# A written-out engine order, rewritten for its first third: casts and copies on other engines, transfers and tiles as they were

## The chip, the cores and the metric

The kernel runs on one core of one Trainium2 chip. The metric is device microseconds of that core for one launch; lower is better. The kernel before was timed three times.

## What is computed

Windowed attention with a few global keys, and behind it a two-layer block with a softplus. B, H, S, D are 4, 8, 768, 64; the model width is 512 and the inner width 2048.

```python
scores = scale * q @ k.T + bias          # bias: -slope[h] * distance
keep   = (key < 8) | (0 <= row - key < 96)
a      = softmax(where(keep, scores, -1e9))
x      = (a @ v) as [3072, 512]          # heads side by side
h      = x @ w_in                        # [3072, 2048]
g      = max(h, 0) + log1p(exp(-|h|))    # softplus
out    = g @ w_out                       # [3072, 512], float32
```

## The kernel before

**Work and names.** The 3072 tokens are 24 blocks of 128. Two neighbouring blocks are a unit (12 units, `UNITS`, line 147); two blocks in the order of work are also a group g of 256 tokens for the second half (12 groups). Every piece of work is a small operation with a name:

- `ldq`, `ldk`, `ldv`, `win`, `wout` load a unit's q, k, v or a piece of the weights (all on SP's queue but the two halves of the first q, on ACT's). `castq`, `castk`, `castv` (lines 650 to 710) and `cin`, `cout` (line 644) turn what was loaded from float32 into bf16. `castv2.11` is the last quarter of unit 2's v.
- `trq`, `trk` transpose a unit's q and k: units 0 to 2 on TensorE with copies `cpq`, `cpk` behind it (lines 777 to 821), later units by a DMA from SP's queue (lines 823 to 838).
- Block n: `sc` scores (line 950), `z` adds the bias on DVE (line 976), `ex` is the exponential on ACT (line 983), `pv` the product with v (line 1002, in two parts), `nm` divides by the sum (lines 1013 and 1014), `xt` transposes the result (line 1033 on TensorE with the copy `xc`, line 1038, for blocks 0 to 5, and from block 6 on a DMA from SP's queue, line 1045). `gk` and `gv` (lines 846 to 871) copy the keys and values of the 8 global tokens into the previous block's tile, where `pv` reads them; `gv4.0` and `gv4.1` do so for block 4.
- Group g: `a{g}.{0..7}` is the product with w_in (line 1060, eight matmuls each), `e` the exponential (line 1075), `ln` the logarithm of 1 + e (line 1086). For groups 0 and 1 the product with w_out is `b{g}.{half}.{0,2,..14}` (line 1107, two matmuls each) and `oc` copies it out. From group 2 on it is made of seven products of half size, `b{g}.1` to `b{g}.7` (line 522), from differences of g (`ka`, line 452) and from sums of weights (`ws{p}.{j}`, line 417, 20 of them, made once).
- `fill0` to `fill34` (line 1234) are matmuls on a blank tile whose result nobody reads.

**What sets the order.** `ORDER` (lines 68 to 145) lists all 1042 operations, each with the letter of its engine (P TensorE, V DVE, A ACT, G POOL, S SP). `Program.in_order` walks through this list and issues each operation; each engine executes its own in that order, and waits where an input is not ready or a buffer is still read. Some operations may stand on more than one engine, and the letter decides:

```python
if alts:
    o.eng = self.placed[name]
    assert o.eng in alts, (name, o.eng)
    o.fn = lambda: fn(o.eng)
assert o.eng == self.placed[name], name
```

**Buffers that the steps below touch.** PSUM has two score buffers (`s_ps`, two banks each) and one bank each in `x_ps`, `o_ps`, `h_ps0`, `h_ps1`. The products `b0.1.*` collect in a bank of the second score buffer, `b0.0.*` in one of the first, so that `b0.1.0` cannot start before `z5.1` has read the scores of block 5 out of it, nor `b0.0.0` before `z5.0` has. There are three `z` buffers, so that `z5.1` also waits for the exponential that reads the buffer it takes.

Of the kernel before, what the change touches and what calls it, by code (L numbers as in the profile page):

```python
# [68 lines left out]
ldv0:S iota:G ldq0.0:A blank:V fill0:P ldk0.0:S table:A ldq0.1:A ident:G dl1a:V fill1:P dl0a:V ldk0.1:S dl0b:V fill2:P
ones:G dl1c:V dl0c:V fill3:P d0:G fill4:P d0e:V ldk1.0:S fill5:P fill6:P biasFalse5:G biasFalse3:V dl1e:V ldq1.0:S  # L70
fill7:P biasTrue0:V biasTrue3:A biasFalse1:G biasTrue5:V ldq1.1:S fill8:P biasTrue6:A ident_q:G fill9:P biasTrue7:V
castv0.01:A ldk1.1:S biasFalse6:G biasFalse7:V fill10:P biasTrue1:A biasTrue4:V castv0.11:G fill11:P ldv1:S
biasFalse2:V biasFalse0:A fill12:P castq0.0:A fill13:P fill14:P biasFalse4:V ident_p:G castk0.0:V biasTrue2:A fill15:P
# [5 lines left out]
cpk1.0:V fill28:P cpk1.1:A xt1:P cin0:V win6:S fill29:P sc2.0:P cin1:A fill30:P z2.1:V fill31:P win7:S z2.0:V xc1:A
cin3:G castv1.10:V ex2.0:A sc3.0:P fill32:P a0.0:P z3.0:V wout0:S cin2:G wout1:S pv2.0:P fill33:P e0.0:A a0.1:P  # L80
nm2.0:V wout2:S castq2.0:G ex2.1:A z3.1:V castq2.1:G a0.2:P ldv2:S e0.1:A castk2.0:G pv2.1:P castk2.1:V trq2.0:P
e0.2:A nm2.1:V wout3:S trk2.0:P ex3.0:A cin5:G cpq2.0:V xt2:P cpk2.1:V a0.3:P xc2:V cpk2.0:A cpq2.1:V pv3.0:P ex3.1:A
cin4:G fill34:P nm3.0:V sc4.0:P ln0.0:A pv3.1:P gk5:G a0.4:P nm3.1:V cin6:G e0.3:A z4.0:V xt3:P e0.4:A a0.5:P cin7:G
ln0.1:A wout4:S z4.1:V a0.6:P xc3:A cout0:G e0.5:A wout5:S sc5.0:P e0.6:A a0.7:P ex4.0:A z5.0:V cout1:G ldq3:S a1.0:P
e0.7:A ldk3:S z5.1:V b0.0.0:P e1.0:A a1.1:P cout2:V ex4.1:A ws0.4:V b0.1.0:P castv2.11:G castv2.01:A b0.0.2:P wout7:S
castv2.00:V b0.1.2:P e1.1:A gv4.1:G ws0.1:V a1.2:P ln0.2:A pv4.0:P ws0.6:V a1.3:P e1.2:A nm4.0:V cout3:A b0.0.4:P
ws1.1:V pv4.1:P e1.3:A a1.4:P cout4:V wout6:S ln0.3:A ws0.3:V ldv3:S a1.5:P gv5.1:V nm4.1:V ln1.0:A b0.1.4:P cout5:V
xt4:P ex5.0:A b0.0.6:P castq3.0:V b0.1.6:P ws2.6:V b1.0.0:P trq3:S e1.4:A b0.1.8:P ws1.4:V ln1.1:A b1.0.2:P ws1.7:V
b0.0.8:P e1.5:A xc4:V b1.0.4:P ws2.1:V castv2.10:A b0.1.10:P ex5.1:A a1.6:P gv5.0:V cout7:V ldq4:S cout6:V a1.7:P
castk3.0:A ws1.3:V b0.1.12:P e1.6:A trk3.0:S ws0.7:V b0.1.14:P ln1.2:A pv5.0:P ws2.7:G ws2.4:V b0.0.10:P b0.0.12:P  # L90
gk6:A ldk4:S nm5.0:V e1.7:A b1.0.6:P trk3.1:S oc0.1.0:V pv5.1:P ln1.3:A b0.0.14:P castv3.00:G nm5.1:V b1.0.8:P ws2.3:V
oc0.0.0:A b1.0.10:P castv3.01:A xt5:P ldv4:S sc6.0:P xc5:V castq4.0:A gv6.0:V b1.0.12:P gv6.1:V z6.0:V b1.0.14:P
castv3.10:A trq4:S a2.1:P oc1.0.0:A castk4.0:G z6.1:V ex6.0:A a2.0:P ldq5:S ws1.6:G trk4.0:S pv6.0:P ex6.1:A b1.1.0:P
nm6.0:V b1.1.2:P gk8:A gk7:V pv6.1:P e2.0:A ws3.3:V sc7.0:P gv7.1:G e2.1:A nm6.1:V ldk5:S a2.2:P gv7.0:G z7.0:V
ln2.0:A xt6:S a2.3:P castv4.10:G e2.2:A z7.1:V castv3.11:G b1.1.4:P ex7.0:A gv8.1:G b1.1.6:P trk4.1:S gv8.0:V b1.1.8:P
ws3.4:G e2.3:A pv7.0:P ex7.1:A sc8.0:P nm7.0:V st0.0.0:S a2.5:P castq5.0:G z8.0:V ln2.1:A pv7.1:P b1.1.10:P
castv4.01:G trq5:S e2.5:A nm7.1:V a2.4:P castv4.11:G ex8.0:A z8.1:V castv4.00:G a2.7:P xt7:S e2.4:A gk9:G ws3.6:V
ex8.1:A pv8.0:P castk5.0:G b1.1.12:P st0.1.0:S nm8.0:V a2.6:P ldv5:S e2.7:A ws3.7:V ldq6:S ln2.2:A b1.1.14:P trk5.0:S
pv8.1:P oc1.1.0:V sc9.0:P e2.6:A gv9.1:G ws3.1:V a3.1:P ln2.3:A gv9.0:G z9.0:V a3.0:P e3.1:A ka2.6:G z9.1:V b2.3:P
e3.0:A ldk6:S ex9.0:A b2.4:P nm8.1:V gk10:G ex9.1:A ka2.7:V a3.2:P xt8:S pv9.0:P e3.2:A a3.3:P ldv6:S nm9.0:V oe2.a:A  # L100
trk5.1:S ka2.2:V a3.4:P e3.3:A ka2.1:V ln3.0:A pv9.1:P sc10.0:P nm9.1:V gv10.0:G e3.4:A a3.5:P z10.1:V castq6.0:G
xt9:S b2.1:P e3.5:A gk11:G ka2.5:V ldq7:S castv5.00:G ex10.1:A a3.6:P trq6:S oe2.1:V castv5.01:G a3.7:P gv10.1:V
e3.6:A castv6.01:G z10.0:V ln3.1:A b2.5:P castv5.11:G st1.0.0:S e3.7:A ldk7:S b2.2:P castk6.0:V ex10.0:A trk6.0:S
sc11.0:P oe2.c:V a4.0:P castq7.0:G z11.1:V pv10.0:P e4.0:A castv5.10:G b2.7:P nm10.0:V trk6.1:S ln3.3:A castv6.11:G
z11.0:V a4.2:P ln3.2:A pv10.1:P trq7:S a4.1:P gv11.0:G e4.2:A ka3.6:V gv11.1:G b2.6:P e4.1:A st1.1.0:S nm10.1:V
ex11.0:A a4.4:P castv6.00:G ka3.2:V xt10:S castk7.0:G a4.3:P e4.4:A oe2.7:V ldv7:S sc12.0:P e4.3:A ka3.1:G trk7.0:S
pv11.0:P z12.1:V b3.3:P ex11.1:A nm11.0:V a4.5:P ln4.0:A z12.0:V pv11.1:P e4.5:A a4.6:P nm11.1:V ex12.0:A castv6.10:V
# [1281 lines left out]
```

## Time and profile before

| what | value |
|---|---|
| median of 3 runs | 211.15 us (211.12 to 211.19) |
| the profiled execution | 211.24 us, of it 209.3 us from first to last instruction |
| TensorE (PE) busy | 201.7 us of 209.3 |
| ACT, DVE, POOL busy | 169.9, 156.2, 115.8 us |
| longest links of the chain that ended last | `a` products 33%, seven-product `b` 25% of the span |
| the DMA link in that chain | v of unit 2, 11.38 us |

In the profile's rows a line stands for an operation's kind (L644 is a weight cast, L707 a cast of v, L868 `gv`, and so on), buffer numbers are left out, and what is in square brackets is the idle time of the engine ahead of an instruction and what ended it. PEld is the weight load that runs beside the matmuls. SPq rows are issues of DMAs by SP. The span has three stretches: up to about 28 us the weights and the first units arrive and TensorE also does fillers; from there to about 66 us groups 0 to 2 run beside the last weight pieces; behind that, the seven-product groups.

### The profile page before, as it was taken

The page shows a single profiled execution, that of the slowest core. Times are in us where ns is not written, and L with a number is a line of the kernel's source. Part 1 is how long each engine was busy: PE and PEld are TensorE (multiplying, and loading weights), DVE is VectorE, ACT ScalarE, POOL GpSimd, SP SyncE. Part 2 cuts the span into 40 slices and gives each one's busy share as a digit, 9 for nine tenths or more (in the row PEclk, how much of TensorE's full clock was granted, in tenths as well). Part 3 has the DMA queues.
Part 4 walks back from the last instruction along what each step waited for, and adds up shares of the span by engine and source line. Part 5 has one row for each costly group of instructions (what it writes and reads, how often), then busy time and mean ns, then how long its engine had stood idle before and what let it go on. Part 6 is the DMA issues. An engine that isn't in the chain of part 4 may idle for free.

```text
span 209.3 us, 5513 instructions
## 1 busy us (share of the span) xinstructions
PE 201.7 (96%) x2211; PEld 164.8 (79%) x2211; DVE 156.2 (75%) x293; ACT 169.9 (81%) x239; POOL 115.8 (55%) x131
## 2 busy tenths in 40 slices
...
GB/s 175 364 362 388 388 358 360 332 241 209 220 244 206 253 203 308 172 203 302 197 196 255 200 164 232 188 142 125 103 75 43 111 5 129 74 0 0 103 20 182
DMA packets 70649, 40.99 MB, mean 196 GB/s; under 512 B 30432, under 2 KB 62688, under 8 KB 70624
## 3 DMA queue, kind: packets, MB, share of 16 engines
...
HBM read 27.26 MB, written 6.29 MB: 160 GB/s over the span
## 4 chain that ended last, share of the span: by engine, by line
PE 75%; DMA 12%; DVE 4%; ACT 3%; POOL 2%; SPq 1%; issue 1%; DVEq 0%; ACTq 0%; POOLq 0%
PE h_ps L1060 33%; PE o_ps L522 25%; DMA raw<-in_v_dram 7%; DMA raw<-in_moe_w_in_dram 5%; PE x_ps L1002 5%; PE s_ps L950 4%; PE s_ps L1107 2%; PE o_ps L1107 2%; PE x_ps L522 2%; PE s_ps L522 1%; DVE z L976 1%; POOL vb L707 1%; DVE raw L417 1%; ACT vb L707 1%; SPq L640 1%
## 5 line engine op out<-in xcount | busy, mean ns | idle before, releaser
L1060 PE MATMUL h_ps<-XT,w_in_bf 128*128 128x256 bf16 x768 | 94.6, 273 | 0.0
L1060 PEld LDWEIGHTS <-w_in_bf 128*128 128x128 bf16 x768 | 73.1, 98 | 10.9 <-POOL w_in_bf L644 0.3
L1075 ACT ACTIVATE e<-h_ps 128x512 f32<-128x512 f32 x96 | 60.0, 637 | 18.8 <-PE h_ps L1060 18.2
L1086 ACT ACTIVATE g<-e 128x1024 bf16<-128x1024 f32 x48 | 49.6, 1050 | 0.5
L976 DVE TENSOR_TENSOR z<-s_ps,biasA 128x1024 f32<-128x1024 f32 x38 | 45.9, 1219 | 4.3 <-PE s_ps L950 3.4
L983 ACT ACTIVATE pb<-z 128x1024 bf16<-128x1024 f32 (+1 forms) x44 | 43.2, 990 | 1.1 <-DVE z L976 1.0
L452 POOL TENSOR_TENSOR g<-g 128x1024 bf16<-128x1024 bf16 x11 | 23.8, 2171 | 22.0 <-DVE raw L452 21.8
L522 PEld LDWEIGHTS <-g 128*128 128x128 bf16 x320 | 30.8, 98 | 3.7
L452 POOL TENSOR_TENSOR raw<-g 128x1024 bf16<-128x1024 bf16 x9 | 19.6, 2176 | 14.4 <-ACT g L1086 12.9
L522 PEld LDWEIGHTS <-raw 128*128 128x128 bf16 x240 | 22.6, 98 | 2.8
L707 POOL CAST vb<-raw 64x512 bf16<-64x512 f32 x29 | 20.9, 724 | 7.0 <-DMA raw<-in_v_dram 5.8
L522 PE MATMUL o_ps<-raw,raw 128*128 128x256 bf16 x192 | 24.3, 273 | 0.0
L452 DVE TENSOR_TENSOR raw<-g 128x1024 bf16<-128x1024 bf16 x21 | 16.2, 780 | 6.5 <-ACT g L1086 4.1
L1002 PEld LDWEIGHTS <-pb 128*128 128x128 bf16 x352 | 16.6, 98 | 5.3 <-issue 1.9
L522 PE MATMUL o_ps<-raw,g 128*128 128x256 bf16 x160 | 19.6, 273 | 0.0
L868 POOL COPY vb<-vb 4x512 bf16<-4x512 bf16 x21 | 13.8, 657 | 7.8 <-PE x_ps L1002 5.8
L1014 DVE TENSOR_TENSOR xs<-x_ps,rcp 128x256 bf16<-128x256 f32 x40 | 17.0, 425 | 1.4
L1002 PE MATMUL x_ps<-vb,pb 128*128 128x65 bf16 x304 | 16.0, 194 | 1.3 <-POOL vb L868 0.9
L522 PE MATMUL o_ps<-w_out_bf,g 128*128 128x256 bf16 x128 | 15.8, 273 | 0.0
L675 POOL CAST qb<-raw 128x1024 bf16<-128x1024 f32 (+1 forms) x10 | 9.8, 989 | 7.5 <-DMA raw<-in_q_dram 7.3
L1234 PE MATMUL x_ps<-blank 128*128 128x512 bf16 x35 | 12.4, 476 | 1.2 <-DVE blank L1159 1.2
L1013 DVE RECIPROCAL rcp<-x_ps 128x4 f32<-128x4 f32 x40 | 7.1, 177 | 8.5 <-PE x_ps L1002 8.1
...
## 6 DMA issues: line engine op xcount, KB each, us to landing
...
raw<-in_moe_w_in_dram SPq DMA_DIRECT2D x8, 512.0 KB, 10.1
...
```

Source lines behind the costliest of these rows:

```text
L452: (nc.vector if eng == "DVE" else nc.gpsimd).tensor_tensor(dst, a[0], b[0], ALU.subtract)
L522: nc.tensor.matmul(psum(j), lhs[:, f // 2, f % 2, :], w(f), start=(f == 0 and not (chain and j in "267")), stop=(f == 7), skip_group_check ...
L707: copy_on[eng](dst, src)
L868: copy_on[eng](vb_of(prev)[sl, :, 0:D], vb_of(first)[sl, :, 0:D])
L976: nc.vector.tensor_tensor(z, src, bias, ALU.add)
L983: nc.scalar.activation(pb[:, 0:nr, :].rearrange("p (y a) b -> p y (a b)", y=2), src, AF.Exp, scale=1.0 / root_d)
L1002: nc.tensor.matmul(xv[:, h, :], pb[:, 4 * (h % 2) + 2 * part + h // 2 if lone else u_all * (2 * (h % 2) + h // 2) + u, :], vb_of(prev if u ...
L1014: nc.vector.tensor_tensor(xs[:, 4 * part : 4 * part + 4, :], xv[:, :, 0:D], rcp[:][:, :, None].to_broadcast([P, 4, D]), ALU.mult,)
L1060: last = nc.tensor.matmul(hv[:, j, :], w_in_bf[:, m, fb * P : fb * P + P], XT[g % NXG][:, m, :], start=(m == 0), stop=(m == NM - 1),)
L1075: nc.scalar.activation(e[:, p % 2, :, :].rearrange("p j (b t r) -> p (j b) r t", b=2, r=2), hb[:].rearrange("p (a r t) -> p a r t", a=4, r=2),
L1086: nc.scalar.activation(gt[:, 2 * p - 2 : 2 * p + 2, :].rearrange("p a t -> p (a t)"), e[:].rearrange("p a j t -> p (a j t)"), AF.Ln, bias=1.0,
L1234: nc.tensor.matmul(x_ps[:], blank[:, 0:P], blank[:])
```

## The change

The text of `ORDER` is another list for its first 39 lines, and some neighbours are swapped in ten lines further down; all other code is the same. The same 1042 operations stand in it. Up to about block 8 of 24 they come in another order on PE, DVE, ACT and POOL, and 62 of them stand on another engine. SP's own order is the same, operation for operation; on ACT's queue the two halves of the first q change places. All 35 fillers are kept, the first 14 where they were. One line of the list, before and after:

```diff
-ex1.1:A gk4:G ldq2.0:S pv0.0:P fill18:P nm0.0:V fill19:P fill20:P ldq2.1:S fill21:P castq1.0:A pv0.1:P fill22:P
+castv0.10:A win2:S fill17:P fill18:P ex0.1:A castk1.1:G ldq2.0:S sc1.0:P fill19:P ldq2.1:S ex1.1:A pv0.0:P fill20:P
```

The 62 operations that change engines, by kind: 10 biases, both identity permutations, 17 casts of q, k and v, 12 weight casts (`cin0`, `cin1` to POOL, `cin3` to ACT, `cin4`, `cin5`, `cin7` to DVE; `cout2`, `cout4`, `cout5`, `cout6` to POOL, `cout3` to DVE, `cout7` to ACT), 9 copies out of PSUM, 3 `gk` and 3 `gv` copies (`gv4.1` to DVE) and 6 `ws` (`ws0.3`, `ws2.3`, `ws2.4`, `ws3.7` to POOL, `ws1.6`, `ws2.7` to DVE).

On POOL, from `cin4` (the first row) on, before; L852 is `gk5`, the two L644 ahead of L707 are `cout0` and `cout1`, L707 is `castv2.11`, L868 `gv4.1` and L417 `ws2.7`:

```order
L644 CAST w_in_bf<-raw_77 128x2x512
L852 COPY kT_88<-kTa_91 128x4x8
L644 CAST w_in_bf<-raw_67 128x2x512
L644 CAST w_in_bf<-raw_79 128x2x512
L644 CAST w_out_bf<-raw_72 128x1024
L644 CAST w_out_bf<-raw_73 128x1024
L707 CAST vb<-raw_74 64x8x64
L868 COPY vb<-vb 4x8x64
L417 TENSOR_TENSOR raw_73<-raw_77 128x512
```

The same place on POOL after; L852 is `gk5`, L868 is now `gv4.0`, the L644 from raw_72 on are `cout0`, `cout1`, `cout2`, `cout4`, `cout5`, `cout6`, and the L417 between them is `ws0.3`:

```order
L644 CAST w_in_bf<-raw_67 128x2x512
L852 COPY kT_88<-kTa_91 128x4x8
L868 COPY vb<-vb 4x8x64
L644 CAST w_out_bf<-raw_72 128x1024
L644 CAST w_out_bf<-raw_73 128x1024
L417 TENSOR_TENSOR raw_70<-raw_72,raw_73 128x512
L644 CAST w_out_bf<-raw_80 128x1024
L644 CAST w_out_bf<-raw_76 128x1024
L644 CAST w_out_bf<-raw_77 128x1024
L644 CAST w_out_bf<-raw_78 128x1024
L417 TENSOR_TENSOR raw_73<-raw_76,raw_77 128x512 x2
```

Unit 2's v and `gv4.1` have left POOL, and five weight pieces and three `ws` have come to it.

On DVE, around the scores of blocks 4 and 5 (`z4.0`, `z4.1`, `z5.0`, `z5.1` are the four L976), before; L644 is `cout2`, the L417 are `ws0.4`, `ws0.1`, `ws0.6` and L707 is `castv2.00`:

```order
L976 TENSOR_TENSOR z_95<-s_ps_61,biasA 128x1024
L976 TENSOR_TENSOR z_96<-s_ps_62,biasA 128x1024
L976 TENSOR_TENSOR z_94<-s_ps_61,biasA 128x1024
L976 TENSOR_TENSOR z_95<-s_ps_62,biasA 128x1024
L644 CAST w_out_bf<-raw_80 128x1024
L417 TENSOR_TENSOR raw_70<-raw_72,raw_73 128x512
L707 CAST vb<-raw_74 64x8x64
L417 TENSOR_TENSOR raw_70<-raw_72,raw_73 128x512
L417 TENSOR_TENSOR raw_70<-raw_72 128x512
```

The same place on DVE after; the first L644 is `cin7`, L868 is `gv4.1`, the L417 are `ws0.1`, `ws0.6`, the L707 are `castv2.01`, `castv2.00` and then `castv2.11`, the second L644 is `cout3`:

```order
L644 CAST w_in_bf<-raw_79 128x2x512
L976 TENSOR_TENSOR z_95<-s_ps_61,biasA 128x1024
L976 TENSOR_TENSOR z_96<-s_ps_62,biasA 128x1024
L868 COPY vb<-vb 4x8x64
L417 TENSOR_TENSOR raw_70<-raw_72,raw_73 128x512
L976 TENSOR_TENSOR z_95<-s_ps_62,biasA 128x1024
L976 TENSOR_TENSOR z_94<-s_ps_61,biasA 128x1024
L707 CAST vb<-raw_74 64x8x64 x2
L417 TENSOR_TENSOR raw_70<-raw_72 128x512
L644 CAST w_out_bf<-raw_75 128x1024
L707 CAST vb<-raw_74 64x8x64
```

The last w_in piece is now cast on DVE ahead of `z4.0`, and `gv4.1` and `ws0.1` stand between the scores of block 4 and those of block 5, whose second part now comes first.

On PE the order of the named operations, before, from the last w_in piece on: `a0.6 sc5.0 a0.7 a1.0 b0.0.0 a1.1 b0.1.0 b0.0.2 b0.1.2 a1.2 pv4.0 a1.3 b0.0.4 pv4.1`. After: `a0.7 a0.6 a1.1 sc5.0 a1.0 a1.3 b0.1.0 a1.2 b0.0.0 b0.0.2 b0.0.4 b1.0.0 b0.1.2 pv4.0 b0.1.4 b1.0.2 b0.0.6 b0.1.6 pv4.1`. In group 2, before: `a2.1 a2.0 pv6.0 b1.1.0 b1.1.2 pv6.1 sc7.0 a2.2 a2.3`; after: `a2.1 sc6.0 a2.0 a2.3 a2.2 pv6.0 sc7.0 a2.5 pv6.1 b1.1.0`.

More of the change, by code (lines that the diff above doesn't have):

```diff
@@ L68 @@
 ORDER = """
[L69 to L73, printed above, removed]
@@ L74 @@
-ldk2.0:S trq0.0:P castv0.10:A cpq0.0:V trk0.0:P castv0.00:A win0:S sb0.0:P castq0.1:G cpk0.0:V win1:S fill16:P sc0.0:P
-castk0.1:V trq0.1:P trk0.1:P cpq0.1:A sb1.0:P win3:S cpk0.1:V ex0.0:A sc1.0:P castq1.1:G ex0.1:A win2:S fill17:P
-ex1.1:A gk4:G ldq2.0:S pv0.0:P fill18:P nm0.0:V fill19:P fill20:P ldq2.1:S fill21:P castq1.0:A pv0.1:P fill22:P
-ldk2.1:S ex1.0:A nm0.1:V fill23:P trq1.0:P castv1.11:G win5:S xt0:P castk1.1:G pv1.1:P cpq1.1:A fill24:P nm1.1:V
-pv1.0:P xc0:A castk1.0:G fill25:P fill26:P castv1.00:A nm1.0:V win4:S castv1.01:G trk1.0:P cpq1.0:A fill27:P gv4.0:G
@@ L79 @@
[L79 to L107, printed above, removed]
+ldv0:S iota:G ldq0.1:A blank:V fill0:P ldk0.0:S table:A ldq0.0:A ident:G dl0a:V fill1:P dl1a:V ldk0.1:S dl0b:V fill2:P
@@ new lines @@
+ident_q:V dl0c:V fill3:P d0:G fill4:P d0e:V ldk1.0:S fill5:P dl1c:V fill6:P ldq1.0:S dl1e:V fill7:P biasFalse0:V
+biasTrue7:A biasFalse2:V biasFalse4:V ldq1.1:S fill8:P biasTrue2:V biasFalse7:A biasTrue0:V biasTrue1:A fill9:P
+biasTrue5:V biasFalse5:A biasFalse1:V ldk1.1:S castv0.01:G castv0.11:A fill10:P biasFalse6:A fill11:P ldv1:S
+biasTrue4:A fill12:P castq0.1:G fill13:P castv0.00:A ones:G castk0.0:V trq0.1:P fill14:P biasFalse3:V biasTrue6:V
+fill15:P cpq0.1:V fill16:P castq0.0:G sb0.0:P biasTrue3:V trk0.0:P ldk2.0:S castk0.1:A trq0.0:P cpk0.0:V win0:S
@@ new lines @@
+cpq0.0:V trk0.1:P ident_p:V win1:S sc0.0:P castk1.0:V cpk0.1:A castq1.0:G sb1.0:P win3:S ex0.0:A castq1.1:V
+castv0.10:A win2:S fill17:P fill18:P ex0.1:A castk1.1:G ldq2.0:S sc1.0:P fill19:P ldq2.1:S ex1.1:A pv0.0:P fill20:P
+nm0.0:V fill21:P ldk2.1:S fill22:P fill23:P ex1.0:A castv1.11:G castv1.01:V pv1.1:P trq1.0:P castv1.00:G win5:S
+nm1.1:V pv0.1:P fill24:P cpq1.1:A trk1.0:P nm0.1:V cpq1.0:A win4:S fill25:P fill26:P cpk1.1:V gk4:A pv1.0:P cpk1.0:V
+fill27:P fill28:P castv1.10:V sc2.0:P nm1.0:V win6:S xt0:P fill29:P cin1:G z2.1:V fill30:P xt1:P fill31:P z2.0:V xc1:A
@@ new lines @@
+win7:S cin0:G xc0:V ex2.0:A sc3.0:P ex2.1:A pv2.0:P fill32:P wout0:S nm2.0:V cin3:A a0.1:P cin2:G z3.0:V fill33:P
+wout1:S e0.1:A pv2.1:P a0.0:P nm2.1:V ex3.0:A wout2:S z3.1:V castq2.1:G xt2:P ldv2:S a0.3:P castk2.0:A e0.0:A xc2:V
+fill34:P wout3:S castk2.1:V e0.3:A pv3.0:P castq2.0:V a0.2:P ex3.1:A cin5:V trk2.0:P nm3.0:V ln0.0:A trq2.0:P cin4:V
+pv3.1:P cpk2.1:V cpq2.0:A a0.5:P nm3.1:V e0.2:A cin6:G cpk2.0:V xt3:P e0.5:A cpq2.1:V a0.4:P xc3:V cin7:V sc4.0:P
+wout4:S e0.4:A a0.7:P ln0.1:A z4.0:V gk5:G gv4.0:G a0.6:P wout5:S e0.7:A cout0:G z4.1:V a1.1:P e0.6:A cout1:G ldq3:S
@@ new lines @@
+gv4.1:V ex4.0:A sc5.0:P ldk3:S ws0.3:G ws0.1:V a1.0:P e1.1:A z5.1:V gk6:A a1.3:P e1.0:A ex4.1:A z5.0:V cout2:G
+b0.1.0:P wout7:S a1.2:P ln1.0:A castv2.01:V b0.0.0:P castv2.00:V ws0.6:V ln0.2:A b0.0.2:P b0.0.4:P cout3:V cout4:G
+b1.0.0:P ex5.0:A castv2.11:V b0.1.2:P ws1.4:V pv4.0:P e1.2:A b0.1.4:P nm4.0:V wout6:S e1.3:A b1.0.2:P ws0.4:V ldv3:S
+b0.0.6:P ln1.1:A cout5:G b0.1.6:P pv4.1:P a1.5:P ex5.1:A nm4.1:V ws2.6:V b0.1.8:P ln0.3:A xt4:P castq3.0:V a1.4:P
+xc4:A ws1.1:V trq3:S e1.5:A b1.0.4:P ws0.7:V b0.0.8:P gv5.1:A gv5.0:V b0.0.10:P ws2.7:V castv2.10:A a1.7:P e1.4:A
@@ new lines @@
+ws1.3:V ldq4:S castk3.0:V b0.1.10:P cout6:G e1.7:A pv5.0:P trk3.0:S a1.6:P ln1.2:A nm5.0:V ws1.7:V ws2.3:G b1.0.6:P
+e1.6:A b1.0.8:P ws2.1:V cout7:A pv5.1:P ldk4:S b0.1.12:P nm5.1:V b1.0.10:P trk3.1:S castv3.01:A b0.1.14:P ln1.3:A
+ws2.4:G b0.0.12:P oc0.1.0:V xt5:P b0.0.14:P gv6.1:V xc5:A b1.0.12:P castv3.10:G ldv4:S ws1.6:V oc0.0.0:A b1.0.14:P
+gv6.0:V castq4.0:A a2.1:P gv8.0:G trq4:S sc6.0:P e2.1:A castv3.00:G a2.0:P oc1.0.0:A z6.0:V castv3.11:G ldq5:S a2.3:P
+gk8:G e2.0:A z6.1:V castk4.0:G ex6.0:A a2.2:P gk7:G trk4.0:S e2.3:A pv6.0:P gv8.1:G sc7.0:P ex6.1:A nm6.0:V a2.5:P
```

29 lines of the change are left out of this document (21 added, 8 removed).

## Prediction

> **What bounds the kernel now.** I read the busy shares of the page first, then stages, then the chain that ended last and the rows around TensorE's (PE's) idle times.
>
> ```profile
> span 209.3 us, 5513 instructions
> core 0: us, PE busy (x) PEld busy (x) DVE busy (x) ACT busy (x) POOL busy (x), PEclk, DMA share, GB/s
> 20.00:28.00 8.00, 7.73 (x107) 6.57 (x105) 6.69 (x16) 7.18 (x11) 6.54 (x9) 1.00 1.05 387
> 28.00:36.20 8.20, 7.26 (x68) 5.20 (x67) 6.33 (x9) 7.93 (x13) 5.18 (x5) 1.00 1.09 356
> 53.00:66.00 13.00, 12.60 (x163) 9.28 (x162) 11.67 (x22) 12.94 (x19) 9.61 (x15) 1.00 1.18 206
> 66.00:203.00 137.00, 137.00 (x1545) 120.61 (x1546) 100.62 (x175) 111.56 (x154) 79.73 (x75) 1.00 0.68 149
> ```
>
> From 66 to 203 us PE is never idle: it is the bound, and the order there is nearly untouched. So the change can only move the moment at which PE has got through the work of blocks 0 to 8. Ahead of 28 us PE is fed by arriving weights; from 28 to 36 us it stands idle for 0.94 us, from 53 to 66 for 0.40.
>
> The first of these, in the timeline:
>
> ```profile
> 33.51 0.42 DVE L707 CAST vb<-raw 64x512 bf16<-64x512 f32 x1
> 33.51 2.09 POOL L707 CAST vb<-raw 64x512 bf16<-64x512 f32 x1 [2.26 <-DMA raw<-in_v_dram]
> 33.84 0.68 DVE L417 TENSOR_TENSOR raw<-raw,raw 128x512 bf16<-128x512 f32 x1
> 34.44 0.68 DVE L417 TENSOR_TENSOR raw<-raw 128x512 bf16<-128x512 f32 x1
> 35.55 0.61 POOL L868 COPY vb<-vb 4x512 bf16<-4x512 bf16 x1
> 36.21 0.37 PE L1002 MATMUL x_ps<-vb,pb 128*128 128x65 bf16 x7 [0.95 <-POOL vb L868]
> ```
>
> `pv4.0` waits 0.95 us for `gv4.1`, which stands behind `castv2.11` on POOL. That cast takes 2.09 us, while DVE runs a cast and two `ws` back to back until 35.12; the same cast on POOL elsewhere takes 0.61:
>
> ```profile
> 14.44 0.61 POOL L707 CAST vb<-raw 64x512 bf16<-64x512 f32 x1
> ```
>
> POOL was shut out for some 1.5 us. This is the one big stall, and POOL against DVE will decide the new places too.
>
> **The front: no gain ahead of 28 us.** The weights land when they did (SP's order is the same), and these rows mark the landings:
>
> ```profile
> 24.71 1.04 POOL L644 CAST w_in_bf<-raw 128x1024 bf16<-128x1024 f32 x1 [0.33 <-DMA raw<-in_moe_w_in_dram]
> 27.26 2.07 PE L1060 MATMUL h_ps<-XT,w_in_bf 128*128 128x256 bf16 x16
> 27.41 1.04 POOL L644 CAST w_in_bf<-raw 128x1024 bf16<-128x1024 f32 x1 [0.30 <-DMA raw<-in_moe_w_in_dram]
> 28.50 0.55 PEld L1060 LDWEIGHTS <-w_in_bf 128*128 128x128 bf16 x6 [0.27 <-POOL w_in_bf L644]
> 29.27 0.63 PE L950 MATMUL s_ps<-qT,kT 64*128 64x128 bf16 x16
> 15.69 0.68 DVE L644 CAST w_in_bf<-raw 128x1024 bf16<-128x1024 f32 x1
> ```
>
> PE's prices, from the chain:
>
> ```profile
> 69.61 0.87 PE h_ps L1060 x8
> 70.48 0.24 PE x_ps L1002 x8
> 72.71 0.55 PE s_ps L950 x16
> 42.69 0.43 PE s_ps L1107 x2
> ```
>
> After, `cin4` and `cin7` stand on DVE, 0.68 us instead of 1.04. `a0.5` can start at 24.71 + 0.68 = 25.39; behind it come `a0.5`, `xt3`, `a0.4`, `sc4.0` (0.87 + about 0.24 + 0.87 + 0.55 = 2.53), so 27.92. `a0.7` needs `cin7`: 27.41 + 0.68 = 28.09. PE has then done the same work as before at 28.1, where the second `a` of the row at 27.26 began. All that moved ahead of this (identities, biases, first casts) has the wait for 25.39 and 28.09 as its cover; I cost it at nothing, and if a chain of copies overruns the cover it costs what it overruns, a few tenths.
>
> Before, PE then lost twice more: the weight load at 28.50 waited 0.27 for `cin7` inside `a0.6`, which reached the matmuls only in part, and `sc5.0` started at 29.27 where back-to-back work (28.13 + 0.87) would have let it start at 29.00. That is one 0.27, counted once. After, `a0.7` and `a0.6` run from 28.09 to 29.83 and `sc5.0` stands one `a` later: nothing waits. Term 1: **-0.27 us**.
>
> **The stall at `pv4.0`.** Unit 2's v still lands at 33.4. After, its quarters for block 4 are cast on DVE behind `z5.0`, `gv4.0` and `gv4.1` are done before it lands, and `castv2.11` is not needed by block 4. On PE `pv4.0` comes after `a1.3`, `b0.1.0`, `a1.2`, `b0.0.0`, `b0.0.2`, `b0.0.4`, `b1.0.0`, `b0.1.2`, at about 36.6; the DVE casts end near 35. Term 2: **-0.95 us**.
>
> What is late next is on DVE: `gv4.1` and `ws0.1` now stand ahead of `z5.1`, which frees the bank for `b0.1.0`.
>
> ```profile
> 29.78 1.23 DVE L976 TENSOR_TENSOR z<-s_ps,biasA 128x1024 f32<-128x1024 f32 x1 [0.63 <-ACT e L1075]
> 30.21 1.04 POOL L644 CAST w_out_bf<-raw 128x1024 bf16<-128x1024 f32 x1 [0.40 <-DMA raw<-in_moe_w_out_dram]
> 39.09 0.29 DVE L868 COPY vb<-vb 4x512 bf16<-4x512 bf16 x1
> 58.34 1.28 POOL L417 TENSOR_TENSOR raw<-raw,raw 128x512 bf16<-128x512 f32 x1
> ```
>
> `z4.0` and `z4.1` run from 28.1 to 28.1 + 2 x 1.23 - 0.1 = 30.4. `gv4.1` is ready then, but `cout1` took POOL at 30.21 and holds it until 31.25. If DVE comes next: `gv4.1` 0.29 and `ws0.1` 0.68 end at 32.1 (each overlaps the next by 0.08), `z5.1` 1.23 ends at 33.25. PE reaches `b0.1.0` after `a0.7`, `a0.6`, `a1.1`, `sc5.0`, `a1.0`, `a1.3` = 5 x 0.87 + 0.55 = 4.90 behind 28.09, with about 0.1 of hand-over: 33.1. Term 3: **+0.15 us**. Two rows tell whether DVE comes next. Against it:
>
> ```profile
> 62.43 1.97 DVE L417 TENSOR_TENSOR raw<-raw 128x512 bf16<-128x512 f32 x1
> 62.55 0.38 POOL L855 COPY kT<-kTa 128x16 bf16<-128x16 bf16 x2
> 62.82 1.03 POOL L687 CAST kb<-raw 128x1024 bf16<-128x1024 f32 x1
> ```
>
> a `ws` began at 62.43 and ended 64.40, 0.54 after POOL's cast ended: it lost to three POOL instructions in a row. For it:
>
> ```profile
> 176.86 2.12 POOL L452 TENSOR_TENSOR g<-g 128x1024 bf16<-128x1024 bf16 x1
> 177.49 2.04 DVE L452 TENSOR_TENSOR raw<-g 128x1024 bf16<-128x1024 bf16 x1
> 178.95 2.57 POOL L452 TENSOR_TENSOR raw<-g 128x1024 bf16<-128x1024 bf16 x1
> ```
>
> here DVE ended at 179.53, 0.55 after the first POOL instruction, and the second one was the slower by 0.45: DVE came next. POOL's instructions there are full-width and long, as `cout1` and `ws0.3` are, so I take the second case. The Trainium skill, page "SBUF — State Buffer", section "Who interferes with whom", says that DVE and POOL share a port pair as an exclusive lock, that the one who issues first holds it for its whole instruction, and that the other blocks fully. The 2.09 us row agrees; by that rule the waiting DVE copy issued before `ws0.3` and goes next, which gives the same +0.15, but the rows at 62.43 differ from it, and they decide that the other outcome stays a rival.
>
> **From 36 to 66 us.** PE's work is the same in sum and stands 1.07 us earlier. The casts of w_out on POOL (1.04 instead of 0.68) come in time for their `b`: `cout2`, behind `ws0.3` (32.1 + 1.28 + 1.04), is done at 34.4 for `b0.0.4` at 35.4. The last two pieces were cast like this before:
>
> ```profile
> 44.12 1.27 DVE L644 CAST w_out_bf<-raw 128x1024 bf16<-128x1024 f32 x2
> 54.71 0.27 PE x_ps L1002 x8
> ```
>
> that is, the last one until 45.39. On POOL `cout6` may start as late as 45.0 and still serve `b0.1.12`, due at 46. The 0.40 us of idle time from 53 to 66 could go as well, since two more `a` now stand ahead of `pv6.0`. But then SP comes in:
>
> ```profile
> DMA to landing us min/median/max: 3.9/3.9/3.9
> 59.56 1.04 POOL L675 CAST qb<-raw 128x1024 bf16<-128x1024 f32 x1
> 60.62 1.23 SPq L837 DMA_TRANSPOSE qT<-qb  x1
> 61.95 1.25 SPq L1045 DMA_TRANSPOSE XT<-xs  x1
> 65.94 0.50 PE L1060 MATMUL h_ps<-XT,w_in_bf 128*128 128x256 bf16 x3
> ```
>
> The first row is from the answer for the tile XT from 61 to 67 us, where `xt7` is the one DMA. Issued at 61.95, it landed 3.9 us later, near 65.9, and group 3's first `a` started at 65.94, with no slack. `xt7` stood in SP's queue behind the transpose of unit 5's q (60.62), and that waited for `castq5.0` on POOL, which ended at 60.60. So PE gains at 66 us only what POOL and SP gain. On POOL, `castq5.0` comes after `pv6.1` with, before, five copies of 0.61, one `ws` of 1.28 and itself 1.04 (5.4 us) between; after, two copies, the `ws` and itself (3.5 us). `pv6.1` itself, before at 54.7 (the row above), stands three `a` later and two `b` earlier: 54.7 + 3 x 0.87 - 2 x 0.43 - 1.07 = 55.4. So `castq5.0` ends at about 59, 1.5 earlier, of which SP, busy with the transposes ahead, passes on about 1.1. Term 4, the gain that SP lets through: at least term 1 to 3, so **0**. Its bounds: the whole 1.07 lost, or 0.40 more won.
>
> Sum: -0.27 - 0.95 + 0.15 = -1.07 us. The profiled execution took 211.24 us (209.3 span and 1.9 around it) and lies 0.09 above the median 211.15. So 211.15 - 1.07 = **210.1 us**.
>
> **The rivals.**
>
> *POOL keeps DVE out (slower).* If `cout1`, `ws0.3` and `cout2` run on POOL without DVE between, as at 62.43, `gv4.1` starts at 31.25 + 1.28 + 1.04 - 0.1 = 33.5, `z5.1` ends at 33.5 + 0.29 + 0.68 + 1.23 - 0.1 = 35.6, and `b0.1.0` waits 2.5 us instead of 0.15, with all of PE behind it: -0.27 - 0.95 + 2.5 = +1.28, **212.4 us**. It decides against the change once the wait of `b0.1.0` is over 1.2 us, that is, once POOL takes one more instruction than `cout1`. For it: the three rows at 62.43, and POOL's own 1.5 us at 33.51. Chance 0.20.
>
> *The gain is given back at SP (no change).* From `cout1` to the cast of unit 3's v POOL has seven operations instead of three, and `castk4.0` stands behind them; three `ws` and two `gv` of DVE in that place (3 x 0.68 + 2 x 0.29 = 2.6 us) can shut POOL out besides. Then `castk4.0` and the transposes land no earlier than before, PE waits at block 8's scores or at `a3.1` until 65.9, and the time is **211.2 us**. For it: `a3.1` had no slack before. Against: the count for `castq5.0`. Chance 0.22.
>
> *All waits go.* Idle time behind 28.1 us is 0.27 + 0.95 + 0.40 = 1.62: no more can be won there, **209.5 us**. It needs SP to be 1.6 earlier. Chance 0.10.
>
> **How the numbers follow.** The forecast has 0.48, with a range of its own from 209.7 to 210.7 (0.4 more won, or half lost). The likeliest, 210.1, is the prediction. The range runs from 209.5 (all waits gone) to 212.4 (POOL keeps DVE out); outside lie a front that overruns its cover on top of that and a gain ahead of 28 us, together under 0.2. Two per mille (0.42 us, about what a measurement of this kernel can tell from no change): the forecast and the last rival are faster, 0.57 with a little of the second; the second rival makes most of 0.19 the same; the first rival and a front that overruns make 0.24 slower.
>
> **What would show it.** Right: no wait of PE at L1002 near 36 us, `a0.7` at 28.1, `b0.1.0` within 0.3 us of the end of `a1.3`, POOL's `ws0.3` starting only after two DVE instructions, PE idle under 1 us from 28 to 66, group 3's first `a` near 64.9 and PE without idle time behind it. Wrong: a stall of PE on `z` (L976) near 33 to 36 us and `gv4.1` of 2 us or more; or group 3's first `a` at 65.9 again; or PE's sequence reaching `a0.7` after 28.5, which would mean that the front was not covered.

## The result, and the profile after

The changed kernel took 213.32 us (median of 5 runs, 212.34 to 213.80) beside 211.19 (211.12 to 211.39) of the kernel before: a ratio of 1.0097, 95% interval 1.0068 to 1.0126. It is 1.0% slower, where 210.1 and at most 212.4 were forecast. The profiled execution took 213.19, of it 211.4 from first to last instruction.

The stages of the changed kernel; columns as in the prediction (length, busy time of PE, PEld, DVE, ACT and POOL with instruction counts, granted clock, DMA share, GB/s):

```profile
span 211.4 us, 5505 instructions
28.00:36.00 8.00, 7.15 (x71) 5.49 (x71) 7.89 (x9) 7.52 (x12) 5.71 (x7) 1.00 1.09 357
36.00:45.00 9.00, 8.16 (x66) 5.09 (x66) 8.87 (x15) 7.36 (x11) 4.81 (x4) 1.00 1.03 290
45.00:53.00 8.00, 7.00 (x59) 4.23 (x57) 7.89 (x13) 7.01 (x10) 7.77 (x7) 1.00 0.72 182
53.00:66.00 13.00, 12.90 (x162) 9.57 (x162) 11.24 (x21) 12.07 (x18) 7.59 (x13) 1.00 1.24 218
66.00:70.00 4.00, 2.92 (x44) 2.58 (x43) 3.95 (x6) 3.31 (x5) 3.37 (x4) 1.00 0.61 155
```

DVE is busy 24.65 of the 25 us from 28 to 53, and PE loses 0.8 to 1.0 us in each of the first three stages and 1.08 behind 66 us. Every wait of PE over 0.3 us behind 28 us, from the timeline; in brackets what ended it:

```profile
34.00 0.39 PE L1107 MATMUL s_ps<-w_out_bf,g 128*128 128x512 bf16 x1 [0.80 <-DVE z L976]
40.40 0.40 PE L1002 MATMUL x_ps<-vb,pb 128*128 128x65 bf16 x8 [0.79 <-DVE xs L1014]
50.71 0.38 PE L1033 MATMUL x_ps<-ident,xs 128*128 128x128 bf16 x4 [0.94 <-DVE xs L1014]
68.01 1.91 PE L1060 MATMUL h_ps<-XT,w_in_bf 128*128 128x256 bf16 x16 [1.08 <-DMA XT<-xs]
```

They are `b0.1.0`, `pv4.1`, `xt5` and group 3's first product `a3.1`. The waits of before (0.27 + 0.95 + 0.40 = 1.62 by the prediction's count) are gone; these four make 3.61. The difference, 1.99, is nearly all of what `a3.1` moved (65.94 to 68.01, 2.07), and behind it nothing more changes: the span grew by 2.1.

The first three waits end with DVE. DVE and POOL around `b0.1.0` (`gv4.1`, `ws0.3`, `ws0.1`, `cout2`; the two `z` of block 5 follow in one row):

```profile
30.23 0.89 DVE L868 COPY vb<-vb 4x512 bf16<-4x512 bf16 x1
30.94 1.32 POOL L417 TENSOR_TENSOR raw<-raw,raw 128x512 bf16<-128x512 f32 x1
31.15 1.66 DVE L417 TENSOR_TENSOR raw<-raw,raw 128x512 bf16<-128x512 f32 x1
32.20 1.50 POOL L644 CAST w_out_bf<-raw 128x1024 bf16<-128x1024 f32 x1
32.73 2.34 DVE L976 TENSOR_TENSOR z<-s_ps,biasA 128x1024 f32<-128x1024 f32 x2
```

`ws0.1` takes 1.66 instead of 0.68: it waits out POOL's `ws0.3`. So `z5.1` ends at 33.94 and not at 33.25. Ahead of `pv4.1` (`cout4` and `cout5` on POOL; `ws0.6`, `cout3`, `castv2.11`, `ws1.4`, `nm4.0` on DVE):

```profile
35.80 3.44 POOL L644 CAST w_out_bf<-raw 128x1024 bf16<-128x1024 f32 x2 [2.10 <-DMA raw<-in_moe_w_out_dram]
35.89 0.68 DVE L417 TENSOR_TENSOR raw<-raw 128x512 bf16<-128x512 f32 x1
36.49 0.68 DVE L644 CAST w_out_bf<-raw 128x1024 bf16<-128x1024 f32 x1
37.20 1.15 DVE L707 CAST vb<-raw 64x512 bf16<-64x512 f32 x1
38.38 1.41 DVE L417 TENSOR_TENSOR raw<-raw,raw 128x512 bf16<-128x512 f32 x1
39.92 0.42 DVE L1014 TENSOR_TENSOR xs<-x_ps,rcp 128x256 bf16<-128x256 f32 x1
```

`castv2.11` takes 1.15 instead of 0.42 and `ws1.4` 1.41 instead of 0.68, and `nm4.0`, for which PE waits, stands behind both. Ahead of `xt5` (`ws2.3` and `ws2.4` on POOL; `ws1.7`, `ws2.1`, `nm5.1` on DVE):

```profile
44.76 4.80 POOL L417 TENSOR_TENSOR raw<-raw,raw 128x512 bf16<-128x512 f32 x2
47.21 1.22 DVE L417 TENSOR_TENSOR raw<-raw 128x512 bf16<-128x512 f32 x1
48.35 1.75 DVE L417 TENSOR_TENSOR raw<-raw,raw 128x512 bf16<-128x512 f32 x1
50.23 0.42 DVE L1014 TENSOR_TENSOR xs<-x_ps,rcp 128x256 bf16<-128x256 f32 x1
```

The same again: `ws1.7` and `ws2.1` lose 0.54 and 1.07. With `gv4.1` (0.60), `gv5.0` (0.84) and some smaller ones DVE loses 6.4 us of this kind from 28 to 53 us; the seven operations that came to POOL there (four weight casts, not the five of the section on the change, and three sums) would have cost it 7 x 0.68 = 4.8.

The wait at `a3.1` ends with a DMA. `pv6.1` on PE, and SP's issues behind it (`xt6`, `trk4.1`, a store, `trq5`, `xt7`):

```profile
58.24 0.41 PE L1002 MATMUL x_ps<-vb,pb 128*128 128x65 bf16 x8
59.35 1.19 SPq L1045 DMA_TRANSPOSE XT<-xs  x1
60.59 1.28 SPq L830 DMA_TRANSPOSE kT<-kb  x1
61.93 0.57 SPq L1139 DMA_DIRECT2D out_dram<-osb  x1
62.60 1.30 SPq L837 DMA_TRANSPOSE qT<-qb  x1
64.00 1.21 SPq L1045 DMA_TRANSPOSE XT<-xs  x1
DMA to landing us min/median/max: 4.0/4.0/4.0
```

SP issues them back to back from the moment at which `nm6.1` is done (59.32, behind `pv6.1` at 58.24). `xt7` lands 4.0 us after its issue (last row, for the tile XT from 63 to 69 us), at 67.97, while PE is through with its work at 66.93.

### The profile page after: what moved, and what is told of

Its sections match the earlier page's. It is cut to its first block, busy times and chain, and to the rows that moved or that the text cites. A ratio compares the mean times of both kernels' runs of the same rounds, so it can differ in the third digit from the quotient of the medians.

```text
span 211.4 us, 5505 instructions
## 1 busy us (share of the span) xinstructions
PE 201.1 (95%) x2203; PEld 164.4 (78%) x2211; DVE 164.3 (78%) x300; ACT 167.7 (79%) x236; POOL 120.3 (57%) x127
## 4 chain that ended last, share of the span: by engine, by line
PE 70%; DMA 13%; DVE 12%; issue 2%; SPq 1%; ACTq 0%; POOL 0%; DVEq 0%; ACT 0%
PE h_ps L1060 32%; PE o_ps L522 25%; DMA raw<-in_moe_w_in_dram 8%; DVE raw L417 4%; PE s_ps L950 4%; PE x_ps L1002 4%; DVE z L976 3%; DMA raw<-in_q_dram 3%; DMA XT<-xs 2%; PE x_ps L522 2%; PE s_ps L522 1%; PE o_ps L1107 1%; DVE vb L707 1%; DVE vb L868 1%; DVE xs L1014 1%
## 5 line engine op out<-in xcount | busy, mean ns | idle before, releaser
L976 DVE TENSOR_TENSOR z<-s_ps,biasA 128x1024 f32<-128x1024 f32 x38 | 45.9, 1217 | 3.6 <-PE s_ps L950 3.5
L707 POOL CAST vb<-raw 64x512 bf16<-64x512 f32 x27 | 19.1, 708 | 6.6 <-DMA raw<-in_v_dram 5.6
L452 DVE TENSOR_TENSOR raw<-g 128x1024 bf16<-128x1024 bf16 x21 | 17.1, 822 | 6.5 <-ACT g L1086 4.1
L868 POOL COPY vb<-vb 4x512 bf16<-4x512 bf16 x21 | 14.8, 705 | 8.9 <-PE x_ps L1002 4.6
L675 POOL CAST qb<-raw 128x1024 bf16<-128x1024 f32 (+1 forms) x9 | 9.3, 1035 | 6.1 <-DMA raw<-in_q_dram 5.9
L1234 PE MATMUL x_ps<-blank 128*128 128x512 bf16 x32 | 11.5, 477 | 1.2 <-DVE blank L1159 1.2
```

Source lines behind the costliest of these rows:

```text
L452: (nc.vector if eng == "DVE" else nc.gpsimd).tensor_tensor(dst, a[0], b[0], ALU.subtract)
L707: copy_on[eng](dst, src)
L868: copy_on[eng](vb_of(prev)[sl, :, 0:D], vb_of(first)[sl, :, 0:D])
L976: nc.vector.tensor_tensor(z, src, bias, ALU.add)
L1234: nc.tensor.matmul(x_ps[:], blank[:, 0:P], blank[:])
```

## Experiments

The first has no edit, and the second leaves the list as it is; all others are edits of the list; a letter behind the colon is the engine. The kernel before took 211.31 to 211.35 us beside them.

**The changed kernel again**, for a second trace.

> The changed kernel once more, for its time beside the same kernel before as the other runs and for a second trace. Theory (the waits sit where the written order puts DVE beside POOL, so they come back at the same places with somewhat other sizes): TensorE waits again at b0.1.0 (0.3 to 1.2), pv4.1 (0.4 to 1.2), xt5 (0.5 to 1.3) and for xt7 (0.7 to 1.4), and nowhere else behind 28 us by over 0.3; 213.3 us (212.3 to 213.9). Rival (the waits of the first trace were one execution's bad luck): other places, or less than 2.0 in sum.

213.30 us (213.03 to 213.53), ratio 1.0086 (1.0052 to 1.0120). The waits of PE:

```profile
34.10 0.39 PE L1107 MATMUL s_ps<-w_out_bf,g 128*128 128x512 bf16 x1 [0.80 <-DVE z L976]
40.49 0.40 PE L1002 MATMUL x_ps<-vb,pb 128*128 128x65 bf16 x8 [0.78 <-DVE xs L1014]
50.80 0.38 PE L1033 MATMUL x_ps<-ident,xs 128*128 128x128 bf16 x4 [0.95 <-DVE xs L1014]
68.25 1.91 PE L1060 MATMUL h_ps<-XT,w_in_bf 128*128 128x256 bf16 x16 [1.22 <-DMA XT<-xs]
```

The same places, to 0.01 us but for the DMA. In these two executions DVE and POOL were served in the same turn at every one of these places, so the waits are not one execution's bad luck.

**POOL's seven operations emptied.** Engines and order as changed; the seven write only the first column of each row, and the products read another weight piece or sum in their place, so that part of the weights is left out:

```diff
-copy_on[eng](dst, raw)
+copy_on[eng](dst[:, :, 0:1], raw[:, :, 0:1])      # cout2, cout4, cout5, cout6
-tensor_tensor(dst, a, b, fn)
+tensor_tensor(dst[:, :, 0:1], a[:, :, 0:1], b[:, :, 0:1], fn)      # ws0.3, ws2.3, ws2.4
```

> The changed kernel, every order and engine as it is, but the seven operations that POOL got between 28 and 53 us (cout2, cout4, cout5, cout6, ws0.3, ws2.3, ws2.4) write only the first column of each row; the products read another weight piece or sum in their place, so part of the weights is left out. DVE's own work is the same. Theory (the waits from 28 to 53 us come from POOL's work through DVE, which is shut out for 6.4 us there): DVE's stretches fall under 1 us, the waits at b0.1.0, pv4.1 and xt5 (0.80 + 0.79 + 0.94) go to under 0.4 in sum, group 3 starts near 65.7, still with a wait of 1 us for xt7, 211.0 us. Rival (DVE's list is too long ahead of nm4.0 and nm5.1 whether POOL works or not): over 1.2 us of these waits stay, 212 or more.

```profile
28.00:36.00 8.00, 7.95 (x75) 5.87 (x74) 7.89 (x11) 7.53 (x12) 3.56 (x7) 1.00 1.09 357
36.00:45.00 9.00, 8.95 (x81) 6.13 (x81) 8.18 (x19) 8.88 (x13) 1.16 (x5) 1.00 1.19 286
45.00:53.00 8.00, 7.95 (x73) 4.97 (x73) 6.10 (x11) 7.41 (x12) 4.78 (x9) 1.00 1.14 259
```

PE loses 0.05 per stage instead of 0.85, 0.84 and 1.00; `b0.1.0`, `pv4.1` and `xt5` do not wait, and `a2.1` starts at 49.49 instead of 52.23, where the prediction's steps put it without term 3: 51.28 before, less 0.55 for `sc6.0`, which now stands behind it, less 0.27 and 0.95, is 49.51. 210.63 us (210.31 to 213.25; two of twelve times are 213.2), ratio 0.9995 (0.9968 to 1.0022). DVE's list is the same, and it loses 1.4 us instead of 6.4 there (I had said under 1), so the three waits are POOL's work, felt through DVE. `a3.1` still waits 0.92 for `xt7`; the profiled execution, at 211.68 one of the longer ones, also waits 0.76 at `pv8.0`.

**The seven back on DVE.** Letters alone: `cout2:G` to `cout2:V`, and likewise `cout4`, `cout5`, `cout6`, `ws0.3`, `ws2.3`, `ws2.4`.

> The changed kernel with seven operations put back from POOL to DVE, at their places in the written order: the weight casts cout2, cout4, cout5, cout6 and the sums ws0.3, ws2.3, ws2.4. Theory (the port): between 28 and 53 us these seven cost DVE more by keeping it out than they save it, 6.4 us of stretched instructions against 4.8 us of work (7 x 0.68). With them on DVE the stretches go to under 1 us, the waits of TensorE at b0.1.0, pv4.1 and xt5 shrink from 0.80 + 0.79 + 0.94 to about 1.1 in sum, the first product of group 3 starts at about 66.6 instead of 68.0, and the time falls by 1.3 us against the changed kernel's 213.3, to 212.0 (211.4 to 212.6). Rival (DVE has too much work there, POOL's help was real): 4.8 us more on an engine that is busy 24.7 of 25 us, TensorE waits longer for nm and z, 214 us or more.

213.42 us (212.78 to 214.22), ratio 1.0102 (1.0085 to 1.0119): between the two, no change against the changed kernel.

```profile
33.81 0.39 PE L1107 MATMUL s_ps<-w_out_bf,g 128*128 128x512 bf16 x1 [0.45 <-DVE z L976]
39.94 0.40 PE L1002 MATMUL x_ps<-vb,pb 128*128 128x65 bf16 x8 [0.53 <-DVE xs L1014]
50.88 0.38 PE L1033 MATMUL x_ps<-ident,xs 128*128 128x128 bf16 x4 [1.07 <-DVE xs L1014]
```

DVE's lost time from 28 to 53 us falls from 6.4 to 2.2, but its work rises by 4.8, and it is busy 24.66 us there, as with POOL at work (24.65). My theory was half right: POOL's work is what hurts, but taking it back gives DVE as much work of its own, and the three waits fall only to 2.05 in sum, not to 1.1. That the sums ahead of `nm4.0` and `nm5.1` are what keeps them late then too is not shown: no run has both changes.

**Three sums later on DVE.** POOL keeps its work:

```diff
-gv4.1:V ws0.1:V z5.1:V z5.0:V castv2.01:V
+gv4.1:V z5.1:V z5.0:V ws0.1:V castv2.01:V
-castv2.11:V ws1.4:V nm4.0:V ws0.4:V
+castv2.11:V nm4.0:V ws1.4:V ws0.4:V
-ws1.7:V ws2.1:V nm5.1:V
+ws1.7:V nm5.1:V ws2.1:V
```

> The changed kernel with three sums on DVE written later, each behind the operation that TensorE waited for: ws0.1 behind z5.0, ws1.4 behind nm4.0, ws2.1 behind nm5.1. POOL keeps all its work. Theory (the waits are made by what stands ahead of z5.1, nm4.0, nm5.1 on DVE while POOL holds it up): b0.1.0 starts at 33.2 instead of 34.0, pv4.1 and xt5 wait under 0.4 each, group 3's first product starts 1.6 to 2.4 us earlier, near 66, and the time is 211.3 (210.8 to 211.9). Rival 1 (the stretch only moves to the next DVE instruction that TensorE waits for): under 0.8 us are won, 212.5 or more. Rival 2 (SP sets the start of group 3 whatever happens before): the waits ahead go and the wait for xt7 grows by as much, 213.3.

211.20 us (eight of twelve times 210.68 to 211.94, four 213.38 to 213.66), ratio 1.0024 (0.9991 to 1.0058). The median is 2.1 below the changed kernel's, but a third of the executions took as long as it did; by the ratios, which go by means, 0.6 to 0.7% are won, about 1.4 us. What is left of PE's waits behind 28 us:

```profile
40.53 0.38 PE L1033 MATMUL x_ps<-ident,xs 128*128 128x128 bf16 x4 [0.42 <-DVE xs L1014]
65.65 1.03 PE L1060 MATMUL h_ps<-XT,w_in_bf 128*128 128x256 bf16 x8 [1.10 <-DMA XT<-xs]
```

For the common group the theory holds (only `xt5` waits a little longer than the 0.4 I had said), and both rivals fall: DVE still loses over 3 us from 28 to 53 us, but it hardly hits what PE waits for. Run once more for the upper group of times:

> The run with DVE's order once more, the same kernel: its times fell into two groups before, near 210.9 and near 213.5. Theory (which of DVE and POOL is served first at an instruction's end varies from one execution to the next, and one lost turn moves others): an execution of the upper group shows a chain of stretched DVE instructions at places where the lower one has none; one of the lower group shows the same stretches as the first profile.

210.95 us (210.72 to 213.13), ratio 1.0000 (0.9973 to 1.0028); the profiled execution was again of the lower group and had the same waits (0.47 and 1.12). What makes the upper group stays open.

**Group 2's new order alone.** The list of before up to `a2.1`, the changed one from there.

> The kernel before up to a2.1, and from there the changed kernel's order: what the rewritten group 2 costs or brings alone. Theory (the new order puts pv6.1 behind three more products and sc7.0, and group 3's first product cannot start earlier than 9.8 us after pv6.1 because of SP's transposes): pv6.1 at 56.4, group 3 at 66.2 with a wait of TensorE of 0.7, against 65.94 before: 0.0 to 0.5 slower, 211.6. Rival (TensorE alone sets it): the 0.4 us of idle time from 53 to 66 go, group 3 starts at 65.5, 210.9.

212.30 us (212.02 to 214.82), ratio 1.0057 (1.0032 to 1.0082): slower, by more than I expected. `pv6.1` and `a3.1`:

```profile
57.00 0.41 PE L1002 MATMUL x_ps<-vb,pb 128*128 128x65 bf16 x8
66.82 1.36 PE L1060 MATMUL h_ps<-XT,w_in_bf 128*128 128x256 bf16 x11 [1.08 <-DMA XT<-xs]
```

9.82 us apart, as in the changed kernel (58.24 to 68.01: 9.77) and in the run with DVE's order (55.85 to 65.65: 9.80). The rule holds; I had `pv6.1` 0.6 too early.

**The other half**, DVE's order of above up to `a2.1` and from there the list of before.

> The other half: the changed kernel with the three later sums up to a2.1, and from there the order of the kernel before. Theory: a2.1 starts at 50.4 (sc6.0 stands ahead of it again), and group 2 takes what it took before, 14.7 us, since pv6.1 is early again: group 3 starts at 65.1 with under 0.2 us of waiting, against 65.65 in the run with DVE's order and 65.94 before: 210.4 us. Rival (the transposes of group 3's input have other feeders and land at 65.6 or later anyway): 211.0 or more.

211.02 us (210.86 to 212.60), ratio 0.9995 (0.9979 to 1.0012): the rival's time, 0.6 above mine. `a3.1` starts at 65.65 without a wait for `xt7`, so the new order is what makes that wait; but PE waits earlier instead, for the exponential `ex6.0`, and `a3.1` is no earlier than with the new order (65.65 both times). So group 2's new order costs 1.0 us behind the order of before and nothing that shows behind DVE's order. The wait for `ex6.0`:

```profile
53.16 0.42 PE L1002 MATMUL x_ps<-vb,pb 128*128 128x65 bf16 x8 [0.84 <-ACT pb L983]
```

**SP's order around `xt7`.** `trk4.1` ahead of `xt6`, `trq5` and the store behind `xt7`, `castv4.01` behind `nm7.1`:

```diff
-xt6:S trk4.1:S st0.0.0:S trq5:S xt7:S
+trk4.1:S xt6:S xt7:S trq5:S st0.0.0:S
-castv4.01:V nm7.1:V
+nm7.1:V castv4.01:V
```

> The changed kernel with SP's order changed around xt7: the transpose trk4.1 ahead of xt6, trq5 and the store st0.0.0 behind xt7; on DVE nm7.1 ahead of castv4.01. Theory (the 1.08 us wait at group 3's first product is the queue of SP between xt6 and xt7): xt7 is issued right behind nm7.1, at about 63.1 instead of 64.0, lands at 67.1 instead of 68.0, and the wait of TensorE falls to 0.2: 212.4 us, 0.9 less than the changed kernel. Rival (transposes land one after the other however early they are issued, or xt7 then stands behind trk4.1 in the DMA engines): xt7 lands within 0.3 us of where it did and the time stays at 213.3.

215.44 us (214.06 to 216.54). `xt7` was issued at 63.36 and landed at 65.78, earlier than I had said, and `a3.1` did not wait. But the queue behind it came late, and the scores of block 10 waited for it:

```profile
76.21 0.62 PE L950 MATMUL s_ps<-qT,kT 64*128 64x128 bf16 x16 [0.73 <-DMA kT<-kb]
```

This run does not show what SP's order costs by itself, since its edit moves `castv4.01` on DVE as well. Its waits at `pv8.0` (0.37) and `pv9.0` (0.61) end with DVE and come back in the next run, where `trq5` and the store stay ahead of `xt7`.

Two milder versions follow: `trk4.1` ahead of `xt6`, `castq5.0` ahead of `ws3.4` on POOL, `castv4.01` behind `nm7.1`, once on the changed kernel and once with the three later sums; then the latter without moving `castv4.01`.

> The changed kernel with the rearrangement around group 3's input alone (trk4.1 ahead of xt6 on SP, castq5.0 ahead of ws3.4 on POOL, nm7.1 ahead of castv4.01 on DVE); the waits from 28 to 53 us stay. Theory: they and the wait at group 3 add up, so 1.0 us is won: 212.3 (212.0 to 212.7). Rival: no gain, 213.3, or a loss as with trq5 pushed back.

> The three later sums of the run with DVE's order, and a milder rearrangement around the input of group 3 than the one that failed: on SP only trk4.1 ahead of xt6 (into a stretch where SP idles), on POOL castq5.0 ahead of ws3.4, on DVE nm7.1 ahead of castv4.01; trq5 and the store stay ahead of xt7. Theory (the wait at group 3's first product is the length of the chain from nm6.1 over SP's transposes, and it goes without a new one if nothing on SP is pushed back): trq5 is issued about 1.2 us earlier, xt7 lands at 64.1 to 64.6 instead of 65.6, TensorE waits under 0.2 there, 0.9 to 1.1 less than the run with DVE's order alone: 209.9 in its common case, 1.4 below the kernel before. Rival (the wait moves to the next transpose, as it did to the scores of block 10 when trq5 was pushed back): the wait turns up behind 66 us again, 210.8 or more.

> The three later sums on DVE, and of the rearrangement around group 3's input only what does not touch DVE: trk4.1 ahead of xt6 on SP, castq5.0 ahead of ws3.4 on POOL (castv4.01 stays ahead of nm7.1). Theory (the failed runs lost on DVE, where castv4.01 came to lie beside POOL's castk5.0 and cost 1.24 instead of 0.44, with nm8.1 and then the differences of group 2 late behind it): xt7 lands near 63.9, TensorE does not wait at group 3, pv8.0 and pv9.0 wait under 0.2, and at most half of the 1.1 comes back as a wait at b2.1: 210.2 us (209.8 to 210.7), 1.1 below the kernel before. Rival (the 1.1 us of waiting at group 3 was what let DVE catch up; without it TensorE waits for DVE instead): a wait of 0.8 or more at pv9.0 or b2.1, 210.9 or more.

In this order 215.53 (215.21 to 215.69), 212.73 (212.63 to 213.47) and 210.75 us (210.03 to 211.51). The first two miss by 3.2 and 2.8 us: `xt7` no longer holds PE up, but the same three waits come in both, for DVE, at `pv8.0` (0.38 and 0.35), `pv9.0` (0.61) and `b2.1` (1.04). `castv4.01` on DVE in the first, then in the second with the wait at `b2.1`:

```profile
63.41 1.27 DVE L707 CAST vb<-raw 64x512 bf16<-64x512 f32 x1
60.69 1.24 DVE L707 CAST vb<-raw 64x512 bf16<-64x512 f32 x1
75.37 0.83 PE L522 MATMUL o_ps<-raw,raw 128*128 128x256 bf16 x6 [1.04 <-DVE raw L452]
```

The third one:

```profile
60.13 0.45 DVE L707 CAST vb<-raw 64x512 bf16<-64x512 f32 x1
65.38 1.91 PE L1060 MATMUL h_ps<-XT,w_in_bf 128*128 128x256 bf16 x16 [0.77 <-DMA XT<-xs]
```

The second and the third differ in one cast of 0.42 us, written behind `nm7.1` instead of ahead of it: 2.0 us. Beside POOL's `castk5.0` it costs 1.24, and the `z` behind it, `nm8.1` and the differences of group 2 come late. With it back, the wait at `a3.1` shrinks only from 1.10 to 0.77, since `xt7` then lands 4.1 us after its issue (2.5 in the second version, issued 0.6 earlier). Why, these runs do not show; I had said that it lands near 63.9, and it landed at 65.33. The third run's ratio of 0.9975 (0.9962 to 0.9987) makes it faster than both kernels, by 0.6 us against before.

**The prediction's second term alone**: before with `gv4.1:G` made `gv4.1:V`, ahead of `z5.0`.

> The kernel before with one operation moved: gv4.1 from POOL to DVE, ahead of z5.0. It is the second term of the prediction alone. Theory (the term was right and nothing downstream takes it back): the 0.95 us wait at pv4.0 goes, everything behind it on TensorE comes 0.95 earlier, group 3's first product starts at about 65.0, and the time is 210.25 (210.1 to 210.5). Rival (the transposes of group 3's input give it back): the wait at pv4.0 goes, xt7 still lands at 65.9, and the time is 211.1 (within 0.2 us of before).

210.82 us (210.45 to 211.97), ratio 0.9979 (0.9965 to 0.9993): faster than before, by 0.5 and not by 0.95.

```profile
34.84 0.41 PE L1002 MATMUL x_ps<-vb,pb 128*128 128x65 bf16 x8
52.66 0.42 PE L1002 MATMUL x_ps<-vb,pb 128*128 128x65 bf16 x8 [0.46 <-ACT pb L983]
```

`pv4.0` does not wait, `a2.1` comes 0.98 earlier, but `pv6.0` then waits 0.46 for `ex6.0` instead of 0.24, and `a3.1` starts at 65.21, 0.73 earlier.

## Why the prediction was wrong, by its own steps

**The front and term 1 (-0.27): right.** `a0.7` started at 27.96 (28.1 forecast), `sc5.0` at 30.72 (30.7), without a wait.

**Term 2 (-0.95): right.** `pv4.0` did not wait. Alone it was worth 0.73 us at `a3.1`, and 0.5 in the time.

**Term 3 (+0.15): the mechanism was right, the size was not: +0.80.** DVE did come next after `cout1`, with `gv4.1`. The step that failed is "`gv4.1` 0.29 and `ws0.1` 0.68 end at 32.1 (each overlaps the next by 0.08)": I gave DVE two turns in a row. `ws0.1` started 0.03 after the end of `gv4.1`, not 0.08 ahead of it, and POOL's `ws0.3` had gone in between. My own row at 33.51 shows the other case: POOL's cast waits there through two sums of DVE (33.84, 34.44), each of which starts ahead of the end of the instruction before it. The rows at 62.43 and 177.49 that I weighed tell who follows a POOL instruction; the question here was whether DVE keeps the turn between two of its own.

**From 36 to 66 us (0): wrong, +0.79 and +0.94.** "PE's work is the same in sum and stands 1.07 us earlier" was the costliest step. I set POOL's new casts against the moments at which PE needs their results, and they did come in time: no `b` waited for a `cout`. What I did not walk through is what they do to DVE, with `nm4.0` and `nm5.1` standing behind two stretched instructions each. The emptied run shows both sides: with POOL's seven operations out of the way these two waits and that of term 3 are gone and `a2.1` is where the sum has it without them (49.49 and 49.51).

**Term 4 (0): wrong, +1.08.** Two slips. "`pv6.1` ... stands three `a` later and two `b` earlier" left out that `sc7.0` (0.55) had moved ahead of it as well. And I followed `xt7` back to `castq5.0` on POOL, which set it before; after, `castq5.0` was done at 62.29, ahead of SP's turn for it at 62.60, and the chain that decided is `pv6.1`, `nm6.1`, and SP's five issues from `xt6` to `xt7`. It takes 9.8 us, and PE has 8.7 us of work in that place. On the order of before, the new order of group 2 alone costs 1.0 us in the time.

The sum with the measured terms: -0.27 - 0.95 - 0.40 + 0.80 + 0.79 + 0.94 + 1.08 = +1.99. The first two rivals came true in kind, and together: POOL kept DVE out (not for long at one place, but at three), and the transposes gave time back, though by another chain than the one over POOL that I had named. I had weighed them as alternatives to each other, so the range ended where one of them alone would have ended it.
